# Spreading eight attention units over thirty-two steps of a two-layer feed-forward kernel

## The chip, the cores and the metric

The kernel runs on one core of a Trainium2 chip. The metric is the time of one execution on the device, in microseconds (us). The core has five engines that run side by side, each with its own list of instructions in a fixed order: TensorE (PE in the profile; its weight loads are PEld), VectorE (DVE), ScalarE (ACT), GpSimd (POOL) and SyncE (SP), which here only issues DMAs. Engines wait for each other by semaphores.

## The reference

Three layers follow one another: a retention attention over 2 sequences of 768 tokens with 8 heads of 64, then two feed-forward layers (512 to 2048 to 512) over the 1536 tokens.

```python
for t in range(S):
    state = gamma * state + einsum('bhd,bhe->bhde', k[:, :, t], v[:, :, t])
    y[:, :, t] = scale * einsum('bhd,bhde->bhe', q[:, :, t], state)
x = y.transpose(0, 2, 1, 3).reshape(B * S, H * D)
h = x @ w_in;   x = (softplus(h)) @ w_out            # layer 1
h = x @ w2_in;  out = (h * clip(h + 3, 0, 6) / 6) @ w2_out   # layer 2
```

The weights come as float64 words; q, k, v and the output are float32.

## The kernel before

**Attention units.** The attention is computed in 12 units of 128 tokens (6 for each sequence). A unit u has, in the order of the program: `scores(u)` (16 small matmuls into two PSUM banks, then two VectorE products that make the tile `pt`), the DMAs of q, k and v of a later unit (`fetch`), `prepare(u + 1)` (transposes of k and q of the next unit on TensorE, copied by ScalarE; `vs` on GpSimd), `carry(u)` (matmuls with the running state `bd`, and on GpSimd the fading of that state, `fade`), `intra(u)` (matmuls with `pt`; VectorE makes `on`, ScalarE `x_hi`, GpSimd `x_lo`), and `state(u)` (matmuls, then two VectorE adds into `bd`). The last unit of a sequence has no `state` and no `fade`. Units 0 to 3 make the first 512 tokens, units 4 to 7 the next, units 8 to 11 the last.

**Steps.** A feed-forward layer works on three chunks of 512 tokens, and each chunk takes 16 steps, one for each 128 of the 2048 inner columns: 96 steps in all. A step s does `gemm1` (12 matmuls of 128x512, then a chain over ScalarE and VectorE: `e`, `t`, `g`, and the two parts `hi` and `lo`) and `gemm2` of step s - 2 (12 matmuls into four PSUM banks that are held for the whole chunk). Step 0 begins chunk 0 of layer 1, step 16 chunk 1, step 32 chunk 2. Every product is made of three matmuls, as each operand stands as a high and a low part.

**Weights.** `feed(n)` converts the weight tiles up to number n. A tile is fetched by SyncE (`raw`, 512 KB, three buffers), and converted: one ScalarE pass, four VectorE passes (two TENSOR_SCALAR and two SCALAR_TENSOR_TENSOR on `w`), one ScalarE copy (`w_parts`), one GpSimd subtraction (`w_parts`). All 32 tiles of layer 1 are converted during chunk 0; chunks 1 and 2 use them again.

**Order.** All instructions up to the end of unit 3 and the first two conversions are kept in the order of the program on each engine (`nc.on` is set, lines 23 to 39). After that the compiler orders each engine's list as its own model of the work sees fit, within the dependences. The loop that sets where units stand is at lines 141 to 150: one unit ahead of each of the first eight steps.

**PSUM.** There are eight banks; `bank()` (line 126) hands out the one that has been free the longest. While `gemm2` of a chunk holds four, four are left, and a unit asks for six, one after the other.

Of the kernel before, what the change touches and what calls it, by code (L numbers as in the profile page):

```python
# [10 lines left out]
F32 = mybir.dt.float32  # L11
# [5 lines left out]
P = 128  # L17
# [3 lines left out]


class InOrder:
    """The engines; while `on` is set, each runs its instructions in the order of the program."""

    class Engine:
        def __init__(self, owner, engine):
            self.owner, self.engine = owner, engine

        def __getattr__(self, op):  # L30
            def call(*args, **kwargs):
                ins = getattr(self.engine, op)(*args, **kwargs)  # L32
                return self.owner.tc.keep_in_program_order(ins) if self.owner.on else ins
            return call

    def __init__(self, tc):
        self.tc, self.on = tc, True
        for e in ("tensor", "vector", "scalar", "gpsimd", "sync"):
            setattr(self, e, self.Engine(self, getattr(tc.nc, e)))


@with_exitstack
def kernel(ctx, tc, q, k, v, w1_in, w1_out, w2_in, w2_out, tq, tk, tc_, tg, out):
    nc = InOrder(tc)
    B, H, S, D = q.shape
    NT, DM = out.shape
    DFF = w1_in.shape[1]
    NP = H // 2
    KD = DM // P
    NF = DFF // P  # L50
    C = P
    NCH = S // C
    CH = 512
    chunks1 = [(0, 0, 512), (1, 0, 512), (2, 0, 512)]
    chunks2 = [(0, 0, 512), (1, 0, 512), (2, 0, 512)]
    LAG = 2
    EARLY = 4

    tc.nc.scalar.preload_act_table_set("natural_log_exp_and_others")

    xpool = ctx.enter_context(tc.tile_pool(name="xpool", bufs=1))
    x_hi = [xpool.tile([P, KD, CH], F32R, name=f"x_hi{c}") for c in range(NT // CH)]
    x_lo = [xpool.tile([P, KD, CH], F32R, name=f"x_lo{c}") for c in range(NT // CH)]

    win_p = ctx.enter_context(tc.tile_pool(name="win", bufs=NF))
    wout_p = ctx.enter_context(tc.tile_pool(name="wout", bufs=NF))
    psum = ctx.enter_context(tc.tile_pool(name="psum", bufs=1, space=PSUM))
    raw_p = ctx.enter_context(tc.tile_pool(name="raw", bufs=3))
    cv_p = ctx.enter_context(tc.tile_pool(name="cv", bufs=2))

    w_in_t, w_out_t, raws = {}, {}, {}
    words = {0: (w1_in.bitcast(U32), w1_out.bitcast(U32)), 1: (w2_in.bitcast(U32), w2_out.bitcast(U32))}

    def fetch(m, o, f):
        raw = raw_p.tile([P, CH, 2], U32, tag="raw", name="raw")
        src = words[m][o]
        if o:
            nc.sync.dma_start(out=raw.rearrange("p n t -> p (n t)"), in_=src[f * P:(f + 1) * P, :])
        else:
            nc.sync.dma_start(out=raw.rearrange("p (k n) t -> p k (n t)", k=KD),  # L80
                              in_=src[:, 2 * f * P:2 * (f + 1) * P].rearrange("(k p) f -> p k f", p=P))
        raws[m, o, f] = raw

    def convert(m, o, f):
        """float64 words -> float32 -> two float32r parts whose sum it is."""
        raw = raws.pop((m, o, f))
        low, high = raw[:, :, 0], raw[:, :, 1]
        w = cv_p.tile([P, CH], U32, tag="w", name="w")
        mag = w.bitcast(F32)
        nc.scalar.activation(mag, raw.bitcast(F32)[:, :, 1], AF.Abs)  # L90
        nc.vector.tensor_scalar(mag, mag, HIGH_MIN, HIGH_MAX, ALU.max, ALU.min)
        nc.vector.tensor_scalar(w, w, 3, 0x3FFFFFF8, ALU.logical_shift_left, ALU.bitwise_and)
        nc.vector.scalar_tensor_tensor(w, high, 0xC0000000, w, ALU.bitwise_and, ALU.bitwise_or)
        nc.vector.scalar_tensor_tensor(w, low, 29, w, ALU.logical_shift_right, ALU.bitwise_or)
        t = (wout_p if o else win_p).tile([P, 2, CH], F32R, tag="w", name="w_parts")
        nc.scalar.activation(t[:, 0], w.bitcast(F32), AF.Copy)
        nc.gpsimd.tensor_tensor(t[:, 1], w.bitcast(F32), t[:, 0].bitcast(F32), ALU.subtract)
        if o:
            w_out_t[m, f] = t
        else:  # L100
            w_in_t[m, f] = t.rearrange("p a (k n) -> p a k n", k=KD)

    NU = B * NCH
    order = [(0, 0, f) for f in range(EARLY)]
    for f in range(NF):
        order += [(0, 1, f)] + [(0, 0, f + EARLY)] * (f + EARLY < NF)
    order += [(1, 0, f) for f in range(NF)] + [(1, 1, f) for f in range(NF)]
    done = [0, 0]

    def fetch_weights(n):  # L110
        while done[0] < min(len(order), n):
            fetch(*order[done[0]])
            done[0] += 1

    def feed(n):
        """Convert the next weight tiles up to n, and fetch those after them."""
        n = min(n, len(order))
        while done[1] < n:
            fetch_weights(done[1] + (1 if nc.on else 2))
            convert(*order[done[1]])  # L120
            done[1] += 1

    banks = psum.tile([P, 8, CH], F32, name="banks")
    free = list(range(8))

    def bank(hold=False):
        """The bank that has been free the longest; one that is held goes back with release()."""
        i = free.pop(0)
        if not hold:
            free.append(i)  # L130
            return banks[:, i, :]
        return i, banks[:, i, :]

    def release(i):
        free.append(i)

    def first(f):
        return EARLY + 2 * (f + 1) - max(0, f + 1 + EARLY - NF)

    step, last, n_steps = moe(ctx, tc, nc, out, x_hi, x_lo, w_in_t, w_out_t, chunks1, chunks2, NF, KD, DM, CH, LAG, feed, first, bank, release)  # L140
    s = 0
    with ExitStack() as actx:
        unit = attention(actx, tc, nc, q, k, v, tq, tk, tc_, tg, x_hi, x_lo, CH, bank, feed, fetch_weights)
        for u in range(CH // P, NU):
            unit(u)
            step(s)
            s += 1
    while s < n_steps:
        step(s)
        s += 1  # L150


def attention(ctx, tc, nc, q, k, v, tq, tk, tcc, tg, x_hi, x_lo, CH, bank, feed, fetch_weights):
    B, H, S, D = q.shape
    NP = H // 2
    C = P
    NCH = S // C
    START = CH // C

    const = ctx.enter_context(tc.tile_pool(name="const", bufs=1))  # L160
    ld = ctx.enter_context(tc.tile_pool(name="ld", bufs=3))
# [18 lines left out]
    def fetch(u, *which, parts=1):  # L180
        b, i = units[u]
        for nm in which:
            t = ld.tile([P, H, D], F32, tag=nm + "0" * (u < START), name=nm, bufs=START if u < START else 3)
            src = {"q": q, "k": k, "v": v}[nm][b, :, i * C:(i + 1) * C, :].rearrange("h s d -> s h d")
            for j in range(parts):
                hs = slice(j * H // parts, (j + 1) * H // parts)
                nc.sync.dma_start(out=t[:, hs], in_=src[:, hs])
            nat[nm, u] = t
# [14 lines left out]

    def scores(u):
        qT, kT = tr["q", u], tr["k", u]
        pt = wk.tile([P, 2, NP, C], F32, tag="pt" + "0" * (u < START), name="pt", bufs=2)
        sc = [ps(NP, C) for g in range(2)]
        for j in range(NP):
            for g in range(2):
                r = slice(D * g, D * (g + 1))  # L210
                nc.tensor.matmul(sc[g][:, j, :], kT[r, j, :], qT[r, j, :])
        for g in range(2):
            nc.vector.tensor_tensor(pt[:, g], sc[g], tm_sb[:, g], ALU.mult)
        tr["pt", u] = pt
# [11 lines left out]
    def intra(u):  # L226
        b, i = units[u]
        vs, pt, o = tr["vs", u], tr["pt", u], tr["o", u]
# [3 lines left out]
                             start=(i == 0 and h < 2), stop=True, skip_group_check=True)  # L232
        c, at = divmod(u * C, CH)
        hi, lo = x_hi[c][:, :, at:at + C], x_lo[c][:, :, at:at + C]
        on = wk.tile([P, NP, C], F32, tag="on" + "0" * (u < START), name="on", bufs=2)
        nc.vector.tensor_tensor(on, o, tq_sb, ALU.mult)
        nc.scalar.activation(hi, on, AF.Copy)
        nc.gpsimd.tensor_tensor(lo, on, hi.bitcast(F32), ALU.subtract)
# [46 lines left out]
        transposed(u, "q")  # L285
        decayed(u)

    # the first loads are on their way: the tensor engine's clock comes up meanwhile
    idle = ps(NP, C)
    for i in range(16):  # L290
        nc.tensor.transpose(idle[:, i % NP, :], ident, ident)
# [9 lines left out]
        state(u)  # L301
    feed(2)
    nc.on = False
    for u in range(START + 1, START + 3):
        fetch(u, "k", "q", "v")

    def unit(u):
        scores(u)
        if u + 3 < len(units):
            fetch(u + 3, "k", "q", "v")  # L310
        if u + 1 < len(units):
            prepare(u + 1)
        carry(u)
        intra(u)
        state(u)
# [4 lines left out]
def moe(ctx, tc, nc, out, x_hi, x_lo, w_in_t, w_out_t, chunks1, chunks2, NF, KD, DM, CH, LAG, feed, first, bank, release):  # L320
# [35 lines left out]
        g_t[m, ci, f] = hi, lo  # L356

    def gemm2(m, c, ci, *fs):
        """Add the products of the tiles fs to the accumulators of a chunk, one accumulator after the other."""
        xi, o, n = c  # L360
        nb = (DM if m == 0 else n) // P
        if fs[0] == 0:
# [89 lines left out]
```

## Time and profile before

| | |
|---|---|
| three timed runs | 664.98, 667.46 and 668.4 us, median 667.46 us |
| the profiled execution: span from first to last instruction | 665.3 us |
| PE busy | 617.0 us (93%) |
| DVE busy | 441.7 us (66%) |
| ACT busy | 303.9 us (46%) |
| POOL busy | 155.0 us (23%) |

The span is the only time that the profile gives of its own execution; the median of the timed runs is 2.2 us above it. Busy shares are means over stages with different limits: in the first third VectorE is nearly full, later TensorE is.

### The profile page before, as it was taken

The page shows a single profiled execution, that of the slowest core. Times are in us where ns is not written, and L with a number is a line of the kernel's source. Part 1 is how long each engine was busy: PE and PEld are TensorE (multiplying, and loading weights), DVE is VectorE, ACT ScalarE, POOL GpSimd, SP SyncE. Part 2 cuts the span into 40 slices and gives each one's busy share as a digit, 9 for nine tenths or more (in the row PEclk, how much of TensorE's full clock was granted, in tenths as well). Part 3 has the DMA queues.
Part 4 walks back from the last instruction along what each step waited for, and adds up shares of the span by engine and source line. Part 5 has one row for each costly group of instructions (what it writes and reads, how often), then busy time and mean ns, then how long its engine had stood idle before and what let it go on. Part 6 is the DMA issues. An engine that isn't in the chain of part 4 may idle for free.

```text
span 665.3 us, 7761 instructions
## 1 busy us (share of the span) xinstructions
PE 617.0 (93%) x2963; PEld 495.7 (75%) x2963; DVE 441.7 (66%) x615; ACT 303.9 (46%) x513; POOL 155.0 (23%) x126
## 2 busy tenths in 40 slices
PE   8988878688889999999999999889999999999997
PEld 7866656566567888888777778657888888888886
DVE  4698999999995754459999999994232222322223
ACT  3365545445655655567666555443222222222221
POOL 2665666444442000002221223330000000000000
PEclk9997898978989999999999999999999999999999
DMA  9996633241131000002334223300010000000001
GB/s 199 213 258 185 161 110 121 74 153 63 64 100 59 1 0 1 1 0 64 95 96 158 72 87 128 131 29 0 1 63 1 1 0 1 34 30 1 0 1 64
DMA packets 61446, 46.92 MB, mean 71 GB/s; under 512 B 39136, under 2 KB 55776, under 8 KB 61408
## 3 DMA queue, kind: packets, MB, share of 16 engines
q1 hardware_dynamic: 61408, 46.42, 24.6%
q8 instruction: 23, 0.38, 0.2%
q14 instruction: 15, 0.12, 0.1%
HBM read 43.26 MB, written 3.15 MB: 70 GB/s over the span
## 4 chain that ended last, share of the span: by engine, by line
PE 53%; DVE 36%; issue 6%; ACT 4%; POOL 1%; DVEq 0%; ACTq 0%; POOLq 0%
PE banks L32 53%; DVE w L32 23%; DVE g L32 6%; DVE e L32 3%; ACT e L32 1%; DVE pt L32 1%; DVE lo L32 1%; ACT w L32 1%; DVE bd L32 1%; ACT w_parts L32 1%; DVE on L32 1%; DVE x_lo L32 1%; ACT hi L32 0%; POOL w_parts L32 0%; ACT t L32 0%
## 5 line engine op out<-in xcount | busy, mean ns | idle before, releaser
L32 PE MATMUL banks<-x_hi,w_parts 128*128 128x512 f32 x768 | 257.3, 396 | 5.7 <-DVE g L32 5.7
L32 PEld LDWEIGHTS banks<-x_hi,w_parts 128*128 128x128 f32 x768 | 146.5, 191 | 37.6 <-DVE g L32 6.1
L32 PE MATMUL banks<-x_lo,w_parts 128*128 128x512 f32 x384 | 151.7, 395 | 0.0
L32 POOL TENSOR_TENSOR w_parts<-w,w_parts 128x512 fp32r<-128x512 f32 x64 | 92.4, 1444 | 232.4 <-ACT w_parts L32 195.2
L32 PE MATMUL banks<-hi,w_parts 128*128 128x512 f32 x384 | 132.0, 404 | 4.9 <-ACT hi L32 2.9
L32 DVE SCALAR_TENSOR_TENSOR w<-raw,w 128x512 uint32<-128x512 uint32 x128 | 123.4, 965 | 1.7
L32 PE MATMUL banks<-w_parts,hi 128*128 128x512 f32 (+1 forms) x386 | 118.8, 389 | 0.7 <-ACT hi L32 0.7
L32 DVE SCALAR_TENSOR_TENSOR g<-e,banks 128x512 f32<-128x512 f32 x48 | 33.0, 687 | 119.8 <-ACT e L32 119.8
L32 ACT ACTIVATE hi<-g 128x512 fp32r<-128x512 f32 x96 | 60.6, 632 | 113.4 <-DVE g L32 113.3
L32 PEld LDWEIGHTS banks<-hi,w_parts 128*128 128x128 f32 x384 | 73.5, 192 | 26.2 <-ACT hi L32 9.2
L32 ACT ACTIVATE e<-banks,three 128x512 f32<-128x512 f32 x48 | 32.9, 685 | 123.1 <-PE banks L32 123.1
L32 DVE TENSOR_SCALAR w<-w 128x512 f32<-128x512 f32 (+1 forms) x128 | 84.7, 662 | 5.8 <-ACT w L32 4.4
L32 PE MATMUL banks<-lo,w_parts 128*128 128x512 f32 x192 | 78.6, 410 | 9.2 <-POOL lo L32 6.1
L32 PEld LDWEIGHTS banks<-w_parts,hi 128*128 128x128 f32 x386 | 72.1, 188 | 16.7 <-ACT hi L32 2.3
L32 PEld LDWEIGHTS banks<-x_lo,w_parts 128*128 128x128 f32 x384 | 73.3, 191 | 15.1 <-issue 0.3
L32 DVE TENSOR_TENSOR lo<-g,hi 128x512 fp32r<-128x512 f32 x80 | 55.8, 699 | 39.1 <-ACT hi L32 37.9
L32 PE MATMUL banks<-w_parts,lo 128*128 128x512 f32 (+1 forms) x193 | 75.4, 391 | 5.4 <-DVE lo L32 5.4
L32 ACT ACTIVATE w_parts<-w 128x512 fp32r<-128x512 f32 x64 | 40.2, 628 | 51.9 <-DVE w L32 48.5
L32 DVE SCALAR_TENSOR_TENSOR e<-t,e 128x512 f32<-128x512 f32 x48 | 38.1, 794 | 32.5 <-ACT t L32 32.4
L32 PEld LDWEIGHTS banks<-lo,w_parts 128*128 128x128 f32 x192 | 37.0, 193 | 21.9 <-POOL lo L32 8.1
L32 ACT ACTIVATE w<-raw 128x512 f32<-128x512 f32 x64 | 42.4, 662 | 15.2 <-POOL w_parts L32 12.6
L32 PEld LDWEIGHTS banks<-w_parts,lo 128*128 128x128 f32 x193 | 36.2, 188 | 14.9 <-DVE lo L32 7.5
(47 smaller groups left out, 482.5 us busy)
## 6 DMA issues: line engine op xcount, KB each, us to landing
raw<-in_moe_w_in_dram SPq DMA_DIRECT2D x32, 512.0 KB, 3.8
raw<-in_moe_w_out_dram SPq DMA_DIRECT2D x32, 512.0 KB, 3.3
q<-in_q_dram SPq DMA_DIRECT2D x12, 256.0 KB, 5.3
v<-in_v_dram SPq DMA_DIRECT2D x12, 256.0 KB, 5.4
k<-in_k_dram SPq DMA_DIRECT2D x11, 256.0 KB, 4.9
out_dram<-ob SPq DMA_DIRECT2D x11, 256.0 KB, 2.0
k<-in_k_dram SPq DMA_DIRECT2D x2, 128.0 KB, 2.4
tq_sb<-in_tq_dram SPq DMA_DIRECT2D x1, 256.0 KB, 4.4
```

The lines of the kernel that those rows point to most:

```text
L32: ins = getattr(self.engine, op)(*args, **kwargs)
```

## The change

The inner loop now runs four steps behind each unit (`NF * P // CH` is 16 * 128 / 512 = 4), so units 4, 5, 6 and 7 stand ahead of steps 0, 4, 8 and 12 (chunk 0), and units 8, 9, 10 and 11 ahead of steps 16, 20, 24 and 28 (chunk 1). SyncE keeps the order of the program for the whole kernel. The q, k and v of a unit are fetched two units ahead, not three, into two buffers each, not three. `pt` and `on` of units 4 to 11 have one buffer, not two. Text in quotation marks and one comment are taken out, which changes nothing in the program.

```diff
     class Engine:
-        def __init__(self, owner, engine):
-            self.owner, self.engine = owner, engine
+        def __init__(self, owner, engine, sync):
+            self.owner, self.engine, self.sync = owner, engine, sync
         def __getattr__(self, op):
             def call(*args, **kwargs):
                 ins = getattr(self.engine, op)(*args, **kwargs)
-                return self.owner.tc.keep_in_program_order(ins) if self.owner.on else ins
+                return self.owner.tc.keep_in_program_order(ins) if self.owner.on or self.sync else ins
...
-            setattr(self, e, self.Engine(self, getattr(tc.nc, e)))
+            setattr(self, e, self.Engine(self, getattr(tc.nc, e), e == "sync"))
...
         for u in range(CH // P, NU):
             unit(u)
-            step(s)
-            s += 1
+            for _ in range(NF * P // CH):
+                step(s)
+                s += 1
...
-            t = ld.tile([P, H, D], F32, tag=nm + "0" * (u < START), name=nm, bufs=START if u < START else 3)
+            t = ld.tile([P, H, D], F32, tag=nm + "0" * (u < START), name=nm, bufs=START if u < START else 2)
...
-        pt = wk.tile([P, 2, NP, C], F32, tag="pt" + "0" * (u < START), name="pt", bufs=2)
+        pt = wk.tile([P, 2, NP, C], F32, tag="pt" + "0" * (u < START), name="pt", bufs=1 + (u < START))
...
-        on = wk.tile([P, NP, C], F32, tag="on" + "0" * (u < START), name="on", bufs=2)
+        on = wk.tile([P, NP, C], F32, tag="on" + "0" * (u < START), name="on", bufs=1 + (u < START))
...
-    for u in range(START + 1, START + 3):
-        fetch(u, "k", "q", "v")
+    fetch(START + 1, "k", "q", "v")
     def unit(u):
         scores(u)
-        if u + 3 < len(units):
-            fetch(u + 3, "k", "q", "v")
+        if u + 2 < len(units):
+            fetch(u + 2, "k", "q", "v")
```

## Rows read from the trace of the kernel before

**Rows 1.** The page's table of busy tenths: the span in 40 equal slices of 16.6 us each, for TensorE and VectorE, and below them the clock that TensorE was granted.

```profile
PE   8988878688889999999999999889999999999997
DVE  4698999999995754459999999994232222322223
PEclk9997898978989999999999999999999999999999
```

**Rows 2.** Busy time of each engine in stretches of the span, in the order: stretch, its length, then PE, PEld, DVE, ACT, POOL (us and instructions), granted clock, share of the DMA engines, GB/s. The first is the period of one attention unit among units 1 to 3, where TensorE is never idle; the second holds steps 0 to 7 with units 5 to 11, the third steps 8 to 15 without a unit, the last most of chunk 1.

```profile
17.29:22.41 5.12, 5.12 (x57) 4.59 (x56) 2.82 (x5) 1.72 (x4) 3.49 (x4) 1.00 1.15 246
...
42.83:145.24 102.41, 81.23 (x487) 63.02 (x488) 99.23 (x129) 50.90 (x90) 57.56 (x45) 0.88 0.50 144
145.24:206.18 60.94, 51.95 (x203) 39.60 (x202) 57.75 (x73) 35.54 (x63) 28.68 (x20) 0.94 0.28 87
...
206.18:290.00 83.82, 83.82 (x372) 69.34 (x371) 45.88 (x68) 51.53 (x85) 1.30 (x1) 1.00 0.00 1
```

**Rows 3.** TensorE's instructions in order of time within one attention unit: start, duration, engine, line, operation, tiles, shapes, count (line 32 is the helper that records every operation).

```profile
18.38 0.66 PE L32 MATMUL banks<-ident,k 128*128 128x128 f32 x4
...
19.31 1.06 PE L32 MATMUL banks<-qT,bd 128*128 128x128 f32 x8
...
21.32 1.16 PE L32 MATMUL banks<-vs,k 128*128 128x128 f32 x8
22.41 1.16 PE L32 MATMUL banks<-qT,kT 64*128 64x128 f32 x16
```

**Rows 4.** Groups of instructions from 34 to 210 us (chunk 0): busy time and mean ns of one, then the idle time of the engine before them. VectorE's passes over tiles in SBUF, and all of GpSimd.

```profile
L32 DVE SCALAR_TENSOR_TENSOR w<-raw,w 128x512 uint32<-128x512 uint32 x66 | 71.6, 1085 | 1.1
L32 POOL TENSOR_TENSOR w_parts<-w,w_parts 128x512 fp32r<-128x512 f32 x32 | 47.0, 1469 | 36.5 <-ACT w_parts L32 36.4
L32 DVE TENSOR_SCALAR w<-w 128x512 uint32<-128x512 uint32 x33 | 25.1, 761 | 0.5
L32 DVE TENSOR_SCALAR w<-w 128x512 f32<-128x512 f32 x33 | 24.1, 729 | 0.0
L32 POOL TENSOR_TENSOR lo<-g,hi 128x512 fp32r<-128x512 f32 x16 | 22.2, 1386 | 32.5 <-ACT hi L32 17.1 <-issue 15.4
L32 DVE SCALAR_TENSOR_TENSOR e<-t,e 128x512 f32<-128x512 f32 x16 | 14.7, 920 | 2.6 <-ACT t L32 2.6
L32 DVE TENSOR_TENSOR g<-g,e 128x512 f32<-128x512 f32 x16 | 13.1, 818 | 0.1
L32 POOL TENSOR_TENSOR x_lo<-on,x_hi 128x512 fp32r<-128x512 f32 x8 | 11.6, 1453 | 6.5 <-ACT x_hi L32 6.4
L32 POOL TENSOR_TENSOR vs<-v,tk_sb 128x512 f32<-128x512 f32 x6 | 7.6, 1263 | 3.6 <-issue 3.5
L32 POOL TENSOR_TENSOR bd<-bd,tc_sb 64x256 f32<-64x256 f32 x8 | 6.5, 812 | 4.8 <-PE banks L32 4.3 <-DMA raw<-in_moe_w_out_dram 0.2
L32 DVE TENSOR_TENSOR bd<-bd,banks 64x256 f32<-64x256 f32 x10 | 4.1, 412 | 0.2
```

**Rows 5.** The same VectorE groups from 210 to 300 us (chunk 1), where GpSimd does next to nothing.

```profile
L32 DVE SCALAR_TENSOR_TENSOR e<-t,e 128x512 f32<-128x512 f32 x17 | 11.8, 693 | 28.1 <-ACT t L32 28.1
L32 DVE TENSOR_TENSOR g<-g,e 128x512 f32<-128x512 f32 x17 | 11.7, 691 | 0.5
L32 DVE SCALAR_TENSOR_TENSOR w<-raw,w 128x512 uint32<-128x512 uint32 x2 | 1.4, 684 | 0.0
L32 DVE TENSOR_SCALAR w<-w 128x512 uint32<-128x512 uint32 x1 | 0.4, 429 | 0.0
L32 DVE TENSOR_SCALAR w<-w 128x512 f32<-128x512 f32 x1 | 0.4, 428 | 0.2 <-ACT w L32 0.2
```

**Rows 6.** VectorE's conversion passes in the two halves of chunk 0: the first three lines from 42.83 to 145.24 us (seven units among the steps), the last three from 145.24 to 206.18 us (no unit).

```profile
L32 DVE SCALAR_TENSOR_TENSOR w<-raw,w 128x512 uint32<-128x512 uint32 x39 | 43.6, 1118 | 0.5
L32 DVE TENSOR_SCALAR w<-w 128x512 f32<-128x512 f32 x19 | 15.2, 799 | 0.0
L32 DVE TENSOR_SCALAR w<-w 128x512 uint32<-128x512 uint32 x19 | 14.4, 757 | 0.3
...
L32 DVE SCALAR_TENSOR_TENSOR w<-raw,w 128x512 uint32<-128x512 uint32 x25 | 26.3, 1053 | 0.4
L32 DVE TENSOR_SCALAR w<-w 128x512 uint32<-128x512 uint32 x12 | 9.1, 761 | 0.2
L32 DVE TENSOR_SCALAR w<-w 128x512 f32<-128x512 f32 x12 | 7.4, 614 | 0.0
```

**Rows 7.** The start of the steps in order of time: SyncE's DMA issues, and among them the last matmuls of `state(4)` on TensorE, ScalarE's first pass over the third weight tile, and VectorE's first pass over it.

```profile
20.00 1.01 SPq L32 DMA_DIRECT2D k<-in_k_dram  x1
...
23.43 1.09 SPq L32 DMA_DIRECT2D raw<-in_moe_w_in_dram  x1
...
33.12 0.92 SPq L32 DMA_DIRECT2D raw<-in_moe_w_in_dram  x2
33.73 0.94 PE L32 MATMUL banks<-vs,k 128*128 128x128 f32 x7
37.60 0.69 ACT L32 ACTIVATE w<-raw 128x512 f32<-128x512 f32 x1 [2.61 <-DMA raw<-in_moe_w_in_dram]
38.95 0.88 DVE L32 TENSOR_SCALAR w<-w 128x512 f32<-128x512 f32 x2
```

**Rows 8.** Waits from 34 to 210 us: who waited for whom, us in total, times, longest.

```profile
PEld banks L32 <- DVE pt L32: 8.5, 6, 3.6
```

## The prediction

> **What bounds the kernel now.** I read the busy tenths of the page first [rows 1]. VectorE stands at 9 in slices 4 to 12 and TensorE does not; from slice 13 TensorE stands at 9 and VectorE falls to 5. So there are two regimes with a border near 205 us, and the change carries work over this border. The stretches by stage put numbers on it [rows 2]. Through steps 0 to 15, VectorE is busy 99.23 of 102.41 us and 57.75 of 60.94 us, and TensorE has 21 and 9 us to spare. In chunk 1 TensorE is busy all 83.82 of 83.82 us, and VectorE only 45.88. The reader is to see that an instruction of VectorE taken out of chunk 0 shortens it, that an instruction of TensorE put into chunk 1 lengthens it, and that the reverse in either stage costs nothing.
>
> Next I read the groups of chunk 0 beside the same groups of chunk 1 [rows 4, 5]. The second pass over `w` takes 1085 ns in chunk 0 and 684 ns in chunk 1, the two TENSOR_SCALAR passes 761 and 729 ns against 429 and 428 ns. What differs is GpSimd, busy in the one and still in the other. So VectorE in chunk 0 is full partly because GpSimd slows it, and a unit has GpSimd work too (3.49 us beside 2.82 us on VectorE and 5.12 us on TensorE) [rows 2].
>
> **What moves.** Units 4 to 7 stay in chunk 0, ahead of steps 0, 4, 8 and 12. Units 8 to 11 go from chunk 0 into chunk 1. With them go four `scores`, `carry` and `intra`, three `prepare` (that of unit 8 is issued by unit 7) and three `state` (unit 11 is the last of its sequence). Nothing is removed; the first four units and layer 2 keep their work.
>
> **VectorE's own work out of chunk 0.** Four units at 2.82 us [rows 2] are 11.28 us; unit 11 has no two adds into `bd`, 2 x 0.41 us [rows 4]. That is 10.4 us gained.
>
> **GpSimd's work out of chunk 0.** Four `x_lo` at 1.45, three `vs` at 1.26 and six `bd` at 0.81 us [rows 4] are 14.5 us. What that frees on VectorE I bound from two sides. High: over all of chunk 0 the excess of the five slowed groups is 66 x 0.401 + 33 x 0.332 + 33 x 0.301 + 16 x 0.227 + 16 x 0.127 = 53 us [rows 4, 5], against 47.0 + 22.2 + 11.6 + 7.6 + 6.5 = 94.9 us of GpSimd, 0.56 us for each; 14.5 x 0.56 = 8.1 us. Low: compare the half of chunk 0 with units to the half without. The four passes of one tile take (43.6 + 15.2 + 14.4) / 19.25 = 3.80 us with units and (26.3 + 9.1 + 7.4) / 12.25 = 3.49 us without [rows 6]. These 0.31 us over 19.25 tiles are 6.0 us for seven units, 3.4 us for four; as some of it comes back in other passes I take 2.5 us as the low end. Between 2.5 and 8.1 I take the middle, 5 us. VectorE is then relieved by 15.5 us (13 to 18.5), and chunk 0 gets shorter by as much.
>
> The Trainium skill (SBUF — State Buffer, "Who interferes with whom") says that VectorE and GpSimd share a port pair as an exclusive lock, and that the later one blocks for the whole instruction. The trace agrees that the passes with SBUF inputs are slowed and bears out about half of a full block, 0.56 us for each us. With a full block the relief would be 10.4 + 14.5 = 24.9 us.
>
> **TensorE's work into chunk 1.** Four units at 5.12 us [rows 2] are 20.5 us; less one pair of transposes (18.38 to 19.31, 0.93 us) and one `state` (21.32 to 22.41, 1.09 us) [rows 3], 18.5 us. The clock is full in both stages [rows 1, 2], so this price holds. It could be 2.0 us less if the `scores` of unit 8 and a pair of transposes are set into TensorE's gaps at the end of chunk 0. Chunk 1 has no gap to hide it: 18.5 us lost (16.5 to 18.5).
>
> **New waits in chunk 1.** TensorE's list now holds `scores`, `prepare`, `carry` and `intra` among the steps. `carry` writes the bank that `pt` has to be read from first (four free banks, six asked for), and `intra` needs `pt`; behind them in TensorE's list stand the matmuls of the step, on which all waits. Such a wait took 8.5 / 6 = 1.4 us where VectorE was full [rows 8]; in chunk 1 VectorE is busy 55% of the time. Bounds nothing and 1.4 us for each of four units; I take 0.6, in all 2.4 us lost (0 to 5.7). VectorE, ScalarE and GpSimd take their share of the units in chunk 1 into idle time: 45.88, 51.53 and 1.30 us busy of 83.82 [rows 2].
>
> **SyncE in program order, at the start.** Now the third weight tile is issued at 33.12 us and its first pass begins at 37.60 us, after 2.61 us of wait for it [rows 7]. In the new order `fetch(6)` stands ahead of it, and with two buffers k of unit 6 waits for `state(4)`, whose matmuls end at 33.73 + 0.94 = 34.7 us. Behind that wait in SyncE's list are q, v and then this tile. Three such issues take 23.43 - 20.00 = 3.4 us [rows 7], so it goes out at 38.1 us, 5.0 us later, and can be converted near 42.6 us. VectorE would have begun it at 38.95 us; the three passes of step 0 (0.6 us each from start to start) can be drawn into the gap, and the transfers are fewer than now. Of about 4.3 us I count 2.4 us lost (0 to 4.3).
>
> **What I cost at nothing.** Elsewhere in chunk 0, SyncE's list is held up by raw buffers that VectorE is slow to free, not by a `state`; the queued weights are ahead of VectorE. In chunk 1 no weight is awaited until step 32. A unit's q, k and v are asked for four steps before use, 20 us of cover at 83.82 / 372 x 24 = 5.4 us a step [rows 2]; without that cover each unit would stand for a transfer of some 4 us (the raw tile above took 37.6 - 33.1 = 4.5 us). The single `pt` and `on` are written again four steps later, long after their readers.
>
> **Sum.** -15.5 + 18.5 + 2.4 + 2.4 = +7.8 us on the profiled 665.3 us, that is 673.1 us of span; with the 2.2 us by which the median of the runs stands above the span, 675 us. The ends are -18.5 + 16.5 = -2.0 and -13 + 18.5 + 5.7 + 4.3 = +15.5 us.
>
> **The rivals.** *Relief larger than priced (faster).* If each instruction of GpSimd blocks VectorE for its whole length, chunk 0 loses 24.9 us; with 18.5 us for TensorE and 2.4 us for the start that is -4.0 us, and -8.4 us with the gaps of chunk 0 used and the start hidden, so 659 to 663, say 662 us. For it: single passes of 1.7 us where 0.68 would do stand in the lists. Against it: 3.80 against 3.49 us a tile. It decides from a relief of 18.5 + 3.3 = 21.8 us on. Chance 0.2. By the skill's rule of a full block (SBUF — State Buffer, "Who interferes with whom") it is this case.
>
> *The two cancel (no change).* Relief at its high end of 18.5 us against 18.5 us, with the waits drawn into other work: 667 to 670 us, say 668 us. Here too belongs that the change does not do what it says: only SyncE is pinned after unit 3, and the compiler could set the units' work early again. Chance 0.25.
>
> *Each unit stands in TensorE's way (much slower).* The longest wait for `pt` was 3.6 us [rows 8]; four of these in place of 0.6 us each add 12 us: 687 us. Memory that has to be shared while all 32 weight tiles are held would act the same way, by a chain of step passes that wait for a tile of a unit. Chance 0.1.
>
> *The sum as above (slower),* 0.45, with a range of its own of 671 to 681 us.
>
> **How the numbers follow.** A measurement of this kernel can tell about 0.5%, 3.3 us, from no change. Faster by more: 0.2. Within: 0.25. Slower by more: 0.45 + 0.1 = 0.55. The range goes from 661 us, inside the faster rival, to 683 us, the upper end of the sum, and leaves out some of the faster and most of the much slower case.
>
> **What would show it.** Steps right: the border between the regimes moves from 206 us to about 193 us; mean times of the `w` passes in chunk 0 go down a little; chunk 1 grows from 16 x 5.4 = 87 us by 18 to 23 us with TensorE full; a wait of ScalarE or VectorE for the third raw tile near 40 us; waits of TensorE for `pt` of 1 us or less at steps 16, 20, 24 and 28. Wrong would be: a border at 185 us or earlier (relief underpriced), a chunk 1 with TensorE full but grown by less than 16 us, VectorE idle in chunk 0 for weights more than at the start, or chunks that begin where they did.

## Result and the profile after

The changed kernel takes 674.84 us (median; 673.78 to 677.84), the kernel before 666.97 us in the same comparison. The ratio is 1.0132 with a 95% interval of 1.0099 to 1.0165: slower, by 7.9 us. The profiled execution took 674.52 us, with a span of 672.7 us against 665.3 us, and a mean granted clock of 0.969. One execution each of two kernels below (every second step, and unit 5 early, where it is the profiled one) took 1203 to 1204 us and is left out of their times.

The busy tenths of the page, for TensorE, VectorE and the granted clock, answer to [rows 1]; a slice is 16.8 us.

```profile
PE   8968877879879999999999999989999999999997
...
DVE  4679999999956554548999999994242222322223
...
PEclk9988988988889999999999999989999999999999
```

The picture is that of before: VectorE at 9 up to slice 11, TensorE from slice 13 on, with the clock full from there but for one slice far behind. A shift of a few us is less than a slice, so finer cuts are needed. The next two groups cut both executions at the same three places: the end of VectorE's last conversion of chunk 0, the gating pass `e` of step 16, and that of step 32. Columns as in [rows 2]. First before, then after.

```profile
34.00:201.67 167.67, 135.86 (x721) 104.36 (x720) 163.71 (x209) 89.87 (x158) 91.43 (x68) 0.91 0.45 131
201.67:210.84 9.17, 9.17 (x42) 7.57 (x42) 3.98 (x8) 5.40 (x9) 2.60 (x2) 1.00 0.19 57
210.84:295.40 84.56, 84.56 (x375) 69.96 (x374) 46.13 (x68) 51.64 (x85) 1.14 (x1) 1.00 0.00 1
```

```profile
34.00:189.60 155.60, 122.46 (x537) 90.32 (x536) 148.39 (x191) 87.42 (x153) 80.60 (x57) 0.89 0.40 120
189.60:200.74 11.14, 10.49 (x58) 8.78 (x59) 3.93 (x7) 3.61 (x6) 3.73 (x4) 0.85 0.35 71
200.74:303.35 102.61, 102.61 (x539) 84.44 (x539) 55.57 (x85) 56.40 (x94) 9.54 (x10) 1.00 0.10 29
```

The reader sees the whole result in the first column. Conversions end 12.1 us earlier (155.60 against 167.67 us of stretch), and what follows up to step 32 takes 113.75 us in place of 93.73, 20.0 us more, with TensorE full but for 0.65 us. Step 32 is 7.95 us late, and so is the end, by 7.4 us of span. VectorE is busy 15.3 us less in the first stretch and idle 3.2 us more. (The contents of the two first stretches differ by two things that nearly balance: before converts one weight tile more in its stretch, 3.7 us by the means of [rows 4]; after has four more gating passes in its own, 3.2 us.)

VectorE's groups from 34 us to step 16 in the changed kernel answer to [rows 4].

```profile
L32 DVE SCALAR_TENSOR_TENSOR w<-raw,w 128x512 uint32<-128x512 uint32 x64 | 69.1, 1081 | 0.9
L32 DVE TENSOR_SCALAR w<-w 128x512 uint32<-128x512 uint32 x32 | 24.5, 767 | 0.4
L32 DVE TENSOR_SCALAR w<-w 128x512 f32<-128x512 f32 x32 | 18.7, 583 | 0.9 <-ACT w L32 0.9
L32 DVE SCALAR_TENSOR_TENSOR e<-t,e 128x512 f32<-128x512 f32 x16 | 14.7, 919 | 4.7 <-ACT t L32 4.6
L32 DVE TENSOR_TENSOR g<-g,e 128x512 f32<-128x512 f32 x16 | 13.6, 848 | 0.1
```

The second pass over `w` is as slow as before (1081 against 1085 ns); of the two TENSOR_SCALAR passes one is too (767 against 761 ns) and the other is faster (583 against 729 ns). The excess of the five slowed groups over their times in chunk 1 [rows 5] is now 64 x 0.397 + 32 x 0.338 + 32 x 0.155 + 16 x 0.226 + 16 x 0.157 = 47.3 us, against 53 us.

Two places were not as forecast. The first is the start: TensorE's transposes of unit 5's k, SyncE's issues, then VectorE's two waits, in the changed kernel.

```profile
28.74 0.66 PE L32 MATMUL banks<-ident,k 128*128 128x128 f32 x4
...
29.43 0.37 SPq L32 DMA_DIRECT2D k<-in_k_dram  x1
29.89 0.53 SPq L32 DMA_DIRECT2D q<-in_q_dram  x1
31.18 0.37 SPq L32 DMA_DIRECT2D v<-in_v_dram  x1
31.60 1.37 SPq L32 DMA_DIRECT2D raw<-in_moe_w_in_dram  x2
```

```profile
40.77 0.69 DVE L32 SCALAR_TENSOR_TENSOR e<-t,e 128x512 f32<-128x512 f32 x1 [1.88 <-ACT t L32]
...
46.56 0.69 DVE L32 SCALAR_TENSOR_TENSOR e<-t,e 128x512 f32<-128x512 f32 x1 [1.44 <-ACT t L32]
```

k of unit 6 is issued at 29.43 us, as soon as these transposes end (28.74 + 0.66 = 29.40 us) and before `state(4)`, whose matmuls begin at 33.37 us. The third weight tile goes out at 31.60 us, 1.5 us earlier than before [rows 7]. VectorE still idles there, but what it waits for are the steps' own activations.

The second place is unit 8, at the border of the chunks: TensorE's instructions in order of time.

```profile
183.78 1.16 PE L32 MATMUL banks<-qT,kT 64*128 64x128 f32 x16
184.87 0.66 PE L32 MATMUL banks<-ident,k 128*128 128x128 f32 x4
190.25 1.11 PE L32 MATMUL banks<-ident,q 128*128 128x128 f32 x4 [4.72 <-DVE g L32]
191.16 1.91 PE L32 MATMUL banks<-qT,bd 128*128 128x128 f32 x8
...
195.00 1.16 PE L32 MATMUL banks<-vs,k 128*128 128x128 f32 x8
```

TensorE stands 4.72 us within the unit until VectorE has read a bank of step 15, and the eight matmuls behind the stand take 1.91 us where they took 1.06 us [rows 3]. The unit spans 183.78 to 196.16 us, 12.4 us, where one took 5.12 us in [rows 2]. VectorE's list, and then two lines of ScalarE's, show why the bank is late:

```profile
184.62 1.50 DVE L32 TENSOR_SCALAR w<-w 128x512 uint32<-128x512 uint32 x1
186.04 1.28 DVE L32 SCALAR_TENSOR_TENSOR w<-raw,w 128x512 uint32<-128x512 uint32 x2
187.25 0.68 DVE L32 SCALAR_TENSOR_TENSOR e<-t,e 128x512 f32<-128x512 f32 x1
187.85 1.75 DVE L32 SCALAR_TENSOR_TENSOR w<-raw,w 128x512 uint32<-128x512 uint32 x1
189.52 0.68 DVE L32 SCALAR_TENSOR_TENSOR g<-banks,g 128x512 f32<-128x512 f32 x1
```

```profile
183.46 0.64 ACT L32 ACTIVATE hi<-g 128x512 fp32r<-128x512 f32 x1 [1.36 <-DVE g L32]
183.99 0.58 ACT L32 ACTIVATE e<-banks 128x512 f32<-128x512 f32 x1
```

The last conversions of the chunk stand ahead of the pass `g` that frees the bank. ScalarE's list adds to it: the matmuls of step 15's `gemm1` end at 177.4 us, but ScalarE begins the step's chain only at 183.99 us, because passes that wait for VectorE stand first in its list, `hi` of step 14 the last of them. When the conversions are done, VectorE has nothing left to do while TensorE works at the unit.

Units 9 to 11, in chunk 1, behave as hoped: the waits of TensorE from 200 to 300 us that end with `pt` are

```profile
PEld banks L32 <- DVE pt L32: 0.4, 1, 0.4
```

### The profile page after: what moved, and what is told of

It is laid out like the page before. It is cut to its first block, busy times and chain, and to the rows that moved or that the text cites. A ratio compares the mean times of both kernels' runs of the same rounds, so it can differ in the third digit from the quotient of the medians.

```text
span 672.7 us, 7836 instructions
## 1 busy us (share of the span) xinstructions
PE 623.8 (93%) x2963; PEld 498.2 (74%) x2963; DVE 434.8 (65%) x615; ACT 303.9 (45%) x513; POOL 154.1 (23%) x126
## 4 chain that ended last, share of the span: by engine, by line
PE 52%; DVE 32%; issue 8%; ACT 5%; POOL 1%; DMA 1%; SPq 1%; POOLq 0%; DVEq 0%; ACTq 0%
PE banks L32 52%; DVE w L32 21%; DVE g L32 6%; DVE e L32 2%; ACT e L32 1%; ACT w L32 1%; DVE lo L32 1%; ACT hi L32 1%; ACT w_parts L32 1%; DMA q<-in_q_dram 1%; DVE pt L32 1%; POOL w_parts L32 1%; SPq L32 1%; DVE x_lo L32 0%; ACT t L32 0%
## 5 line engine op out<-in xcount | busy, mean ns | idle before, releaser
L32 PE MATMUL banks<-hi,w_parts 128*128 128x512 f32 x384 | 136.1, 415 | 20.5 <-ACT w_parts L32 12.3
L32 DVE SCALAR_TENSOR_TENSOR w<-raw,w 128x512 uint32<-128x512 uint32 x128 | 121.9, 954 | 1.6
L32 DVE TENSOR_SCALAR w<-w 128x512 f32<-128x512 f32 (+1 forms) x128 | 79.3, 621 | 5.9 <-ACT w L32 4.7
L32 DVE TENSOR_TENSOR g<-g,e 128x512 f32<-128x512 f32 x48 | 46.8, 976 | 0.6
```

## Experiments

Theory A: the sum on record, term by term; moving units 8 to 11 costs the net 5 us, the rest of the change little. Theory B: the total is right by other terms: the place of the units within chunk 0, and the order and buffers, have prices of their own. Theory C, for what lies behind [rows 4]: how much of VectorE's time in chunk 0 belongs to GpSimd, and whether that is the lever rather than where the units stand.

**SyncE's order and the smaller buffers alone.** The kernel before with these parts of the change; units ahead of steps 0 to 7.

```
-                return ... if self.owner.on else ins
+                return ... if self.owner.on or self.sync else ins
...
-        if u + 3 < len(units):
-            fetch(u + 3, "k", "q", "v")
+        if u + 2 < len(units):
+            fetch(u + 2, "k", "q", "v")
...
```

> The kernel before with SyncE in program order, two units fetched ahead and the smaller buffers, but the units where they were (one ahead of each of steps 0 to 7). Theory A (the move of units 8 to 11 costs TensorE 18.5 us in chunk 1 and gives VectorE about 13 us net in chunk 0; order and buffers are free): same as before, 665 to 669 us. Theory B (order and buffers make the loss, by late transfers or by tiles that wait for one another): 671 to 676 us.

Measured: 663.11 us, ratio 0.9939 (0.9918 to 0.9959). This part alone makes the kernel 4.0 us faster, below both ranges above; I had counted 2.4 us lost. Here the third weight tile is issued at 30.60 us. VectorE's mean second pass over `w` falls from 1085 to 974 ns, with the same work on GpSimd (34 us to step 16):

```profile
L32 DVE SCALAR_TENSOR_TENSOR w<-raw,w 128x512 uint32<-128x512 uint32 x66 | 63.7, 974 | 0.8
```

Order and buffers were not run apart.

**Units 8 to 11 across the border, 4 to 7 early.** The changed kernel with units 4 to 7 ahead of steps 0 to 3.

```
-        for u in range(CH // P, NU):
-            unit(u)
-            for _ in range(NF * P // CH):
-                step(s)
-                s += 1
+        ahead = {0: 4, 1: 5, 2: 6, 3: 7, 16: 8, 20: 9, 24: 10, 28: 11}
+        while ahead:
+            if s in ahead:
+                unit(ahead.pop(s))
+            step(s)
+            s += 1
```

> The changed kernel with units 4 to 7 ahead of steps 0, 1, 2 and 3 and units 8 to 11 as changed. Theory A': VectorE's gaps of 1.9 and 1.4 us near 40 and 46 us are there because no unit stands near to fill them; with unit 5 at step 1 they close, and the time is 671 to 673 us. Theory C (they come from SyncE's order): the gaps stay, 674 to 676 us.

Measured: 665.82 us, ratio 0.9978 (0.9965 to 0.9992), below both ranges above. The crossing costs 2.7 us over the run above, not 5.4, and the spreading of units 4 to 7, which I had at nothing, costs the other 9.0 us. VectorE's stretches show what the spreading does. First this kernel, then the changed one: 34 to 60 us, 60 to 160 us, 160 us to step 16.

```profile
34.00:60.00 26.00, 21.94 (x146) 16.94 (x146) 23.71 (x39) 15.36 (x29) 12.53 (x10) 0.93 0.63 182
60.00:160.00 100.00, 80.02 (x320) 58.23 (x319) 98.63 (x121) 57.05 (x100) 54.48 (x40) 0.90 0.41 124
160.00:190.96 30.96, 26.29 (x133) 19.91 (x132) 30.83 (x39) 18.49 (x33) 17.23 (x13) 0.94 0.29 77
```

```profile
34.00:60.00 26.00, 18.96 (x72) 13.16 (x71) 21.51 (x32) 15.18 (x28) 11.77 (x9) 0.87 0.52 163
60.00:160.00 100.00, 80.24 (x359) 59.31 (x360) 98.90 (x123) 55.33 (x98) 52.96 (x38) 0.88 0.43 124
160.00:200.74 40.74, 33.75 (x166) 26.64 (x166) 31.91 (x44) 20.52 (x36) 19.61 (x15) 0.92 0.25 72
```

VectorE does the same work up to step 16, 153.2 and 152.3 us. Its idle time is 2.3 + 1.4 + 0.1 = 3.8 us here and 4.5 + 1.1 + 8.8 = 14.4 us in the changed kernel. The 9 us appear as VectorE's idle time, 2.2 us more at the start and 8.7 us more in the stretch that ends at the border. At the border unit 8 goes like this here, on TensorE and then on VectorE:

```profile
181.99 0.66 PE L32 MATMUL banks<-ident,k 128*128 128x128 f32 x4
182.48 0.60 PE L32 MATMUL banks<-ident,q 128*128 128x128 f32 x4
182.92 1.06 PE L32 MATMUL banks<-qT,bd 128*128 128x128 f32 x8
```

```profile
179.49 0.68 DVE L32 SCALAR_TENSOR_TENSOR g<-banks,g 128x512 f32<-128x512 f32 x1
...
188.37 2.67 DVE L32 SCALAR_TENSOR_TENSOR w<-raw,w 128x512 uint32<-128x512 uint32 x2
190.96 0.68 DVE L32 SCALAR_TENSOR_TENSOR e<-t,e 128x512 f32<-128x512 f32 x1
```

`g` of step 15 is through before the unit asks for the bank, TensorE does not stand, and VectorE has conversions left to do under the unit.

**All eight units in chunk 0, every second step.** The changed kernel with two steps behind each unit.

```
-            for _ in range(NF * P // CH):
+            for _ in range(2):
```

> The changed kernel with two steps behind each unit, not four: units 4 to 11 ahead of steps 0, 2, 4 to 14, all in chunk 0. Theory A: nothing crosses from the stage of VectorE to that of TensorE, so 666 to 670 us (up to 3 us for VectorE's gaps at the start). Theory B (spreading, order or buffers lose the time): 672 to 676 us, as the changed kernel.

Measured: 667.41 us, ratio 1.0003 (0.9987 to 1.0019), 4.3 us slower than with the units ahead of steps 0 to 7 and else the same. VectorE is busy as long up to step 16 (160.5 against 160.3 us) and idle 15.3 against 12.3 us. Spreading costs without any crossing.

**Two units across the border.** The changed kernel with units 4 to 9 at every second step, 10 and 11 ahead of steps 20 and 28.

```
...
+        ahead = {0: 4, 2: 5, 4: 6, 6: 7, 8: 8, 10: 9, 20: 10, 28: 11}
...
```

> Units 4 to 9 ahead of steps 0, 2, 4, 6, 8 and 10, only units 10 and 11 in chunk 1 (ahead of steps 20 and 28). Theory A: half of the units cross, so about half of the loss: 669 to 672 us; chunk 1 grows by some 9 to 10 us against before, and the last conversion of chunk 0 ends about 6 us earlier than before. Theory B: 673 to 676 us.

Measured: 668.17 us, ratio 1.0012 (1.0001 to 1.0022), below both ranges above. Two units moved change the time by under 1 us over the run before: chunk 0 up to step 16 gets 8.0 us shorter (209.82 to 201.86), and from there to step 32 it takes 95.41 us in place of 85.09, 10.3 us more.

**Unit 8 a step later.** The changed kernel with units 8 to 11 ahead of steps 17, 21, 25 and 29.

```
...
+        ahead = {0: 4, 4: 5, 8: 6, 12: 7, 17: 8, 21: 9, 25: 10, 29: 11}
...
```

> The changed kernel with units 8 to 11 one step later (ahead of steps 17, 21, 25 and 29). In the changed kernel TensorE stands still 4.7 us in unit 8 until VectorE has read the bank of step 15 (g). Theory A (this wait is only VectorE's end of chunk 0 seen from TensorE): the wait moves to another instruction, 673 to 676 us. Rival (the unit's place makes it): 670 to 672 us.

Measured: 675.58 us, ratio 1.0136 (1.0101 to 1.017). Nothing is won: TensorE stands again, for 3.91 us up to 195.19 us, and VectorE, with its conversions done at 189.95 us, idles under the unit as before.

```profile
195.19 1.11 PE L32 MATMUL banks<-ident,q 128*128 128x128 f32 x4 [3.91 <-DVE g L32]
```

```profile
191.32 0.63 ACT L32 ACTIVATE hi<-g 128x512 fp32r<-128x512 f32 x1 [3.01 <-DVE g L32]
```

No conversion stands ahead of the `g` of step 16 here. ScalarE's list hands the delay on: `hi` of step 15 waits 3.01 us for VectorE, and the chain of step 16 stands behind it.

**Unit 5 early.** The changed kernel with unit 5 ahead of step 1 in place of step 4.

```
...
+        ahead = {0: 4, 1: 5, 8: 6, 12: 7, 16: 8, 20: 9, 24: 10, 28: 11}
...
```

> The changed kernel with unit 5 ahead of step 1 in place of step 4, all else as changed. Theory: VectorE idles at the start of the changed kernel because no unit stands between steps 0 and 4 whose passes it could draw forward (busy 26.8 us from 28 to 60 us against 29.0 with units at steps 0 to 3). With unit 5 at step 1 it is busy 28 to 29 us there, chunk 0 ends 2 to 3.5 us earlier, and the time is 671 to 673 us. Rival: the loss is not at the start but at the border (the stand of TensorE in unit 8 and its low clock); then the time stays at 674 to 676 us.

Measured: 672.96 us, ratio 1.0087 (1.0058 to 1.0116). It points the way of the theory, 1.9 us less than the changed kernel, but the two ratios' intervals overlap. No trace of this kernel is read here.

**Unit 7 early.** The changed kernel with unit 7 ahead of step 9 in place of step 12.

```
...
+        ahead = {0: 4, 4: 5, 8: 6, 9: 7, 16: 8, 20: 9, 24: 10, 28: 11}
...
```

> The changed kernel with unit 7 ahead of step 9 in place of step 12, all else as changed, so that seven steps without a unit stand ahead of unit 8. Theory: TensorE's stand of 4.7 us in unit 8, with the low clock behind it, comes of VectorE's passes that unit 7 pushed into the last steps of chunk 0; without them the stand is under 1 us, unit 8 takes 6 to 8 us and not 12, and the time is 668 to 671 us. Rival: the stand comes of the order of VectorE's list at step 15 alone (conversions of the last weight tiles ahead of the pass that frees the bank); then it stays at 4 to 5 us and the time at 674 to 676 us.

Measured: 673.02 us, ratio 1.0095 (1.0067 to 1.0122), 1.8 us less than the changed kernel, again with overlapping intervals, and in neither range above. The stand in unit 8 is 3.27 us in place of 4.72, not under 1 us, and the unit takes 10.0 us (183.64 to 193.67). My theory of this stand fell: seven steps without a unit do not clear VectorE's list, as conversions stand ahead of step 15's passes here too (the last two ahead of `e` run from 186.12 to 187.40 us). Each of the two single moves gives back about 2 of the 9 us; what the four early units win together beyond that stays open.

**GpSimd's subtraction for layer 1's weights on VectorE.** The kernel before.

```
-        nc.gpsimd.tensor_tensor(t[:, 1], w..., t[:, 0]..., ALU.subtract)
+        (nc.vector if m == 0 else nc.gpsimd).tensor_tensor(t[:, 1], w..., t[:, 0]..., ALU.subtract)
```

> The kernel before with the subtraction that makes the low part of layer 1's 32 converted weight tiles on VectorE, not GpSimd (47.0 us of GpSimd in chunk 0 go, VectorE gets 32 passes of about 0.6 us, 19 us). It prices what one us of GpSimd costs VectorE. At my low end (2.5 us for 14.5, 0.17): VectorE gets 8 us back, so slower, 676 to 680 us. At 0.56 (the mean of chunk 0): 26 us back, 658 to 662 us. At a full block (1.0): 47 us back, 640 to 645 us.

Measured: 651.49 us, ratio 0.977 (0.972 to 0.982). VectorE got 31 passes more in the engine that seemed full, and the kernel is 14.9 us faster than in the same comparison without the edit (666.41 us). That lies between the range for 0.56 us and the one for a full block. VectorE's groups from 34 to 195 us:

```profile
L32 DVE SCALAR_TENSOR_TENSOR w<-raw,w 128x512 uint32<-128x512 uint32 x62 | 48.1, 782 | 0.4
L32 DVE TENSOR_TENSOR w_parts<-w,w_parts 128x512 fp32r<-128x512 f32 x31 | 23.3, 755 | 0.0
L32 DVE TENSOR_SCALAR w<-w 128x512 uint32<-128x512 uint32 x31 | 21.5, 696 | 0.2
L32 DVE TENSOR_SCALAR w<-w 128x512 f32<-128x512 f32 x32 | 19.4, 610 | 1.7 <-ACT w L32 1.7
```

With `e` (816 ns, 16 passes) the excess is now 62 x 0.098 + 31 x 0.070 + 31 x 0.267 + 32 x 0.182 + 16 x 0.123 = 24.3 us, where it was 53: without these 47.0 us of GpSimd [rows 4] it is 28.7 us less, about 0.6 us for each. This is a rough estimate: the new sum has four second passes over `w` fewer and the new passes `w_parts` in it, and GpSimd's `lo` takes 1848 ns now, against 1386.

**GpSimd's passes for units 4 to 11 on VectorE.** The kernel before.

```
-        (nc.vector if u < 2 else nc.gpsimd).tensor_tensor(
+        (nc.vector if u < 2 or u >= START else nc.gpsimd).tensor_tensor(
...
-        nc.gpsimd.tensor_tensor(lo, on, hi..., ALU.subtract)
+        (nc.vector if u >= START else nc.gpsimd).tensor_tensor(lo, on, hi..., ALU.subtract)
...
-            nc.gpsimd.tensor_tensor(s, s, tc_sb[r]..., ALU.mult)
+            (nc.vector if u >= START else nc.gpsimd).tensor_tensor(s, s, tc_sb[r]..., ALU.mult)
```

> The kernel before with the GpSimd work of units 4 to 11 (x_lo, vs, the fading of bd) on VectorE: 25.7 us of GpSimd go, VectorE gets about 11 us. At 0.17 per us: 4 us back, 672 to 675 us. At 0.56: 14 us back, 662 to 665 us. At 1.0: 26 us back, 651 to 654 us.

Measured: 662.6 us, ratio 0.9939 (0.9924 to 0.9955), inside the range for 0.56 us, with the second pass over `w` at 936 ns in place of 1085.

**All of it on VectorE.** Both edits on the kernel before, for both layers, and the subtraction `lo` of chunk 0 too; GpSimd is left with the first four units.

> The kernel before with no work on GpSimd after the first four units (95 us of GpSimd go in chunk 0, VectorE gets 32 + 16 + 8 + 6 passes of 0.6 us and 8 of 0.4 us, 40 us; layer 2's conversions too). At 0.17 per us: slower, 690 us or more. At 0.56: 53 us back, 13 us gained in chunk 0, 652 to 656 us. At 1.0: 95 us back, chunk 0 no longer bound by VectorE alone, 630 us or less.

Measured: 629.57 us, ratio 0.9443 (0.9414 to 0.9472): 37 us faster than before. That is the time that stands above for a full block, but by the traces only 19.5 us of it come from chunk 0 (step 16 at 191.38 us in place of 210.84). Another 17.7 us lie behind step 32 (352.2 us of span in place of 369.9), where layer 2's weights are converted and GpSimd is quiet now too. So the time does not show a full block. The page's busy tenths for TensorE and GpSimd, and VectorE's groups from 34 to 190 us:

```profile
PE   8996999999899999999999999999999999999997
...
POOL 2500000000000000000000000000000000000000
```

```profile
L32 DVE SCALAR_TENSOR_TENSOR w<-raw,w 128x512 uint32<-128x512 uint32 x60 | 40.7, 685 | 0.0
L32 DVE TENSOR_TENSOR w_parts<-w,w_parts 128x512 fp32r<-128x512 f32 x31 | 21.3, 686 | 8.2 <-ACT w_parts L32 8.0
L32 DVE TENSOR_SCALAR w<-w 128x512 f32<-128x512 f32 x31 | 13.0, 421 | 0.2 <-ACT w L32 0.2
```

Every pass has the time that it has in chunk 1 [rows 5], and TensorE is now the full engine of nearly every slice.

**All on VectorE, with SyncE's order and the smaller buffers.**

> The kernel before with the change's SyncE order and its fetch two units ahead with the smaller buffers, units left where they were, and after the first four units all of GpSimd's passes on VectorE. Theory: the 4.0 us of the order and the buffers and the 36.7 us of GpSimd's passes add up as long as VectorE sets the pace: 626 us; as TensorE is then busy 97% of the time, part of the 4 us may find nothing to shorten, so 625 to 630 us. Rival: the 4 us were less contention with GpSimd, which is gone here; then 629 to 631 us, the same as with GpSimd's passes moved alone.

Measured: 627.37 us, ratio 0.9407 (0.9385 to 0.943). The fastest kernel of the study; the order's 4 us have shrunk to 2.2 us, within the range of the first theory; the two ratios' intervals overlap.

**All on VectorE, with the whole change.**

> The changed kernel with all of GpSimd's passes on VectorE after the first four units. Theory: without GpSimd chunk 0 is no longer bound by VectorE but by TensorE, so the units' work taken out of chunk 0 shortens it by TensorE's own 18.5 us and chunk 1 grows by the same; the placing is then worth nothing by itself and only its waits remain: 630 to 640 us. Rival: VectorE, which now has GpSimd's passes too, still sets the pace of chunk 0, and the placing relieves it: 620 to 628 us.

Measured: 635.88 us, ratio 0.9532 (0.9496 to 0.9568): 8.5 us slower than with the units ahead of steps 0 to 7. Up to step 16 it is 5.3 us shorter (182.53 against 187.83 us), and from there to step 32 it takes 101.00 us in place of 84.79. The time is the one that the first theory gave, but chunk 0 loses far less than the 13.4 us that the three units behind step 16 hold of TensorE's 18.5 us (unit 8, 5.12 us, still stands ahead of that step), so its ground, that TensorE alone sets the pace there, is not borne out: VectorE is still busy 124 of 136 us from 34 to 170 us.

## Why the prediction was right, and where its steps were not

The forecast was 675.0 us in a range of 661 to 683, and slower as the likeliest; the kernel takes 674.8 us. The two large sums hold at the places where they were said to. Chunk 0 up to the last conversion was to lose 15.5 - 2.4 = 13.1 us and lost 12.1; TensorE's stretch after it was to gain 18.5 + 2.4 = 20.9 us and gained 20.0. The border, taken at that conversion, moved from 201.67 to 189.60 us; the forecast had 13 us, from 206 to 193. The table gathers what the traces give for each kernel; times are us, the step's time is the start of its gating pass `e` on VectorE, idle and busy are VectorE's from 34 us to step 16, and the excess is worked out as in the prediction.

| kernel | time | step 16 | 16 to 32 | busy | idle | excess |
|---|---|---|---|---|---|---|
| before | 667.0 | 210.84 | 84.56 | 167.7 | 9.2 | 53.0 |
| order and buffers alone | 663.1 | 206.54 | 84.49 | 160.3 | 12.3 | 46.0 |
| and units 8 to 11 across | 665.8 | 190.96 | 102.52 | 153.2 | 3.8 | 49.7 |
| and units 4 to 7 spread: the change | 674.8 | 200.74 | 102.61 | 152.3 | 14.4 | 47.3 |

**VectorE's own work out of chunk 0 (-10.4) and GpSimd's relief (-5).** Up to the last conversion VectorE is busy 15.3 us less, against 15.5. The units' own passes (`pt`, `on`, `bd`) are 10.7 us of it, so the first term holds. The excess fell by 5.7 us, of which 1.3 us belong to the one weight tile that is converted later. But the table takes the second term away from the moved units: the excess falls from 53 to 46 us with order and buffers alone, and does not fall further when units 8 to 11 go (49.7 and 47.3 us), although GpSimd works 10.7 us less (95.0 to 84.2 us up to step 16). Each is one execution, so a few us of it may be chance; that moving the units bought 5 us of relief is not shown. The size was right, the cause was not. What the crossing did do has no term in the prediction: between the second and the third row the way to step 16 gets 15.6 us shorter, and 8.5 us of that is idle time of VectorE.

**The larger relief (the faster rival).** It needed 21.8 us. The excess fell by 5.7 us, so it is out. A block for the whole length of each GpSimd instruction is not what the sums show either: about 0.6 us for each us, where the subtraction was taken away. The Trainium skill (SBUF — State Buffer, "Who interferes with whom") says that a VectorE instruction with two inputs in SBUF contends with a GpSimd instruction that reads SBUF. The runs agree: 1085 ns beside GpSimd, 685 ns without it.

**TensorE's work into chunk 1 (+18.5) and its new waits (+2.4).** Together 20.0 us, measured. The waits for `pt` that I had priced at 0.6 us a unit come to 0.4 us in all for units 9 to 11. Unit 8 is another matter: it lies at the border, where VectorE was still full, and stood 4.72 us for a bank of step 15. I had put unit 8 among the units of chunk 1, and even given it 2 us for gaps of chunk 0 as a bound. Its stand hardly shows in the sum of this stretch, because all but 0.65 us of it falls before VectorE's last conversion ends at 189.60 us. What filled the place of the waits for `pt` is, in the main, the rest of unit 8 behind the stand: it takes 5.9 us (190.25 to 196.16, two matmuls of a step among it), in part at the lower clock, where the prices of [rows 2, 3] give an estimate of 3.5 us. Units 9 and 10 take 5.4 us each (217.66 to 223.06 and 245.01 to 250.42). So the total was right, and the wait in it was another than the one forecast. (The prediction also says that the clock is full in both stages. By [rows 2] it is 1.00 for the unit among units 1 to 3 and in chunk 1, on which the price rests, but 0.88 and 0.94 in chunk 0.)

**SyncE's order at the start (+2.4).** This step failed. k of unit 6 does not wait for `state(4)`: unit 5 is the last of its sequence and has no `state`, so its k buffer comes free with its transposes, and the third weight tile left at 31.60 us, earlier than before. VectorE did lose time at the start (busy 21.51 of 26 us from 34 to 60 us, against 25.70), and more than I counted, 4.2 us. With order and buffers alone it is busy 23.23 us, with the four early units 23.71: so about half of the loss comes with the spreading, which takes the passes of units 5 to 7 away from the first steps.

**What I cost at nothing.** Two entries were wrong, with opposite signs. Order and buffers are worth 4.0 us to the kernel before. The spreading of units 4 to 7 costs 9.0 us: VectorE's work stays, its idle time grows from 3.8 to 14.4 us. I had read "VectorE is full in chunk 0" as if it stayed full wherever the units stand. By the lists it is full where passes of units and conversions lie ready while the steps' chain of activations does not: ahead of steps 0 to 3 the units fill the start, and conversions are left over for the time of unit 8.

So by the runs, taken in this order, the change is -4.0 (order and buffers), +2.7 (the crossing) and +9.0 (the spreading), in all +7.7 us (the +7.9 us above come from another comparison), where the sum on record has +2.4, +5.4 and 0 (-15.5 + 18.5 + 2.4 is the crossing). The total was right in part by luck: these errors cancel. The start of step 16 shows the same: it moves by -4.3, -15.6 and +9.8 us in that order, -10.1 us in all. Why order and buffers speed the passes up, and where some 5 of the 9 us of the spreading go when unit 5 and unit 7 are moved one at a time, stays open.

## What to carry to other kernels

Work moved from a stage bound by one engine into a stage bound by another is paid at full length there, and repaid at home only as far as that engine is truly kept busy: count its idle time at the seams as well as its work. Before moving work between stages, ask why the full engine is full; here 53 of VectorE's 168 us in chunk 0 were another engine's doing, and handing it that engine's passes gained 37 us, 19.5 of them in chunk 0, where the placing lost 8. And check which instruction last reads a buffer for the very unit in question: the last unit of a sequence had none of the reads that the step was built on.

## What the runs showed of the hardware

A pass of VectorE with two inputs in SBUF took 685 ns with GpSimd still and 1085 ns on average beside it; GpSimd's own pass of 1469 ns for the same tile took 686 ns on VectorE. By the estimate from the run with the subtraction on VectorE (about 0.6 us for each us), such a pass on GpSimd cost VectorE about 0.9 us, more than the 0.69 us that the pass itself takes there. That run bears it out: VectorE got 31 passes more, and the kernel became 14.9 us faster.

After TensorE had stood 4.72 us, eight matmuls took 1.91 us that take 1.06 us at the full clock, a factor of 1.8; the clock's two levels are 1.2 and 2.4 GHz, a factor of 2. The granted clock of the stretch from 189.60 to 200.74 us is 0.85, and it is 1.00 again from 200.74 us on.
